# Cosine attention and a gated MLP on one core: loads put behind a reduction, a product moved to VectorE, gates changed, and identity products put between steps

## The chip, the cores and the metric

The kernel runs on one NeuronCore of a Trainium2 chip. Five engines work side by side: TensorE (PE in the profile, with its weight loads as PEld), VectorE (DVE), ScalarE (ACT), GpSimd (POOL) and SyncE (SP), which here issues most DMAs. Each engine works through its own instructions in program order and waits on semaphores for the others. The metric is the device time of one execution in microseconds; less is better. A measurement of this kernel tells a change of about 1% from none.

## The reference

Inputs: `q`, `k`, `v` of 8 batches, 12 heads, 448 positions and 64 features in float32, a scalar `tau` of 0.1, and two weights.

```python
q_n = q / (np.linalg.norm(q, axis=-1, keepdims=True) + 1e-06)
k_n = k / (np.linalg.norm(k, axis=-1, keepdims=True) + 1e-06)
attn = softmax(np.matmul(q_n, k_n.transpose(0, 1, 3, 2)) / tau)
x = np.matmul(attn, v).transpose(0, 2, 1, 3).reshape(3584, 768)
h = x @ w_in                 # 768 x 2048
out = (h * np.cos(h)) @ w_out    # 2048 x 768, float32
```

## The kernel before, in words

**Attention.** Four heads of one batch are a *quad*; there are 24, three to a batch. A quad's q and k are loaded (`load_qk`, L402, on SyncE's queue, 448 KB each, into a ring of three buffers `Qf`, `Kf`), squared and summed (`norm_a`, L510: squares on POOL, sums on DVE), turned into inverse norms and multiplied in (`norm_b`, L514), and transposed by DMA (`turn`, L541). V is loaded on POOL's queue (`load_v`, L408). For each of a quad's seven parts `scores` (L553) does four 64x64 products on TensorE into two PSUM banks, and ACT takes the exponential into `E`. `attend` (L583) multiplies `E` by V; after the seventh part DVE copies the PSUM result into `AVs` (L599), which frees the banks. The division by the row sums comes later. From quad 6 on, two quads at a time are summed by `round_` (L679): `sums` (L644) does it on TensorE, and `invert` (L660) takes 1/sum on ACT by a logarithm and an exponential into `Zs` (L664, L666), copies it by eight small DMAs on SyncE's queue to the partitions where it is needed, `R` (L672), and POOL multiplies `AVs` by `R` into `xT` (L675). Quads 0 to 5 do this in other ways (`spread`, `invert_spread`, `scale_x`: L603, L621, L634).

**MLP.** For each batch `c`, `m1_part` (L687) multiplies the first weight by `xT` (TensorE, 96 products of 448 columns), `m1` (L700) forms h cos h on ACT and DVE, and `m2` (L715) multiplies by the second weight; DVE copies the result to `osb` and SyncE stores it.

**Order.** The front, up to the first batch's `m1`, is written out by hand (L828 to L980). While it is recorded (`P.strict`) every instruction has a key, its number plus an entry of a table `MOVE` (L83), and each engine works in the order of the keys. TensorE's order is that of the keys all through. Behind the front, the other engines' order is chosen by a planner (L97 to L199), which simulates the engines with the durations and latencies written beside each operation. In a batch's `m2` the loop at L1047 alternates between attention of later quads and `m2`: a table `VISITS` (L749) says how many attention steps come next and how many `m2` products behind them, and `LATER` (L760) shifts the place of the attention product of the quad before in a quad's steps. `begin` (L768) is called as a quad's first scores are recorded: it makes the norms and transposes of quad+2, loads quad+4, and makes the squares of quad+3. A load with `after=` waits for the named operation; in the front the loads of quad 5 wait for the third of the four loads of the second weight, `half[3][:1]` (L930). `warm` (L819) issues products of an identity matrix with itself, which compute nothing that is used.

Of the kernel before, what the change touches and what calls it, by code (L numbers as in the profile page):

```python
# [21 lines left out]
class Planner:  # L22
# [13 lines left out]
    def __init__(self):  # L36
        self.ops = []
        self.last_write = {}
        self.readers = {}
        self.strict = False  # L40
        self.tail = {}

    def op(self, eng, dur, fn, r=(), w=(), after=(), dma=None, moves=0, mode="f", chain=None, keep=False, lead=0.0,
           packet=74, lock=False):
        o = Op()
# [3 lines left out]
        o.behind, o.lead, o.packet, o.lock = None, lead, packet, lock  # L49
        o.key = o.i + (self.MOVE.get(o.i, 0) if self.strict else 0)  # L50
        if keep or self.strict and eng in ("act", "dve", "pool", "sp"):
# [20 lines left out]
    def land(self, ring, issued, took, packet):  # L72
        s = max(issued + self.FIRST, self.ring[ring][0])
        for other, (until, theirs) in self.ring.items():
# [21 lines left out]

# [179 lines left out]
def bass_cosine_attention__then__act_gcu_kernel(  # L276
# [63 lines left out]
    def bank(i, n=S, p0=0, p1=128):  # L340
        return PS.ap()[p0:p1, 512 * i:512 * i + n]
# [4 lines left out]
    P = Planner()  # L346
    op = P.op
# [27 lines left out]
    def act(m, dur, fn, r=(), w=(), **kw):  # L375
        table(m)
        return op("act", dur, fn, r=[*r, "table"], w=w, **kw)
# [24 lines left out]
    def load_qk(qd, after=()):  # L402
        return [load_one(qd, w, after=after) for w in range(2)]
# [106 lines left out]
    def norm_a(qd):  # L510
        for w in range(2):
            square(qd, w, "pool")()
# [147 lines left out]
    def invert(quads, bk):  # L660
        z = 0
        np_ = 2 * len(quads)
        zz = Zs[z].ap()[0:32 * np_, :]
        act("exp", 0.44, lambda e: e.activation(zz, bank(bk, S, 0, 32 * np_), ACT.Ln, bias=0.0, scale=1.0),  # L664
            r=whole(bk), w=[("Zs", z)], lead=LEAD)
        act("exp", 0.47, lambda e: e.activation(zz, zz, ACT.Exp, bias=0.0, scale=-1.0), r=[("Zs", z)], w=[("Zs", z)], lead=LEAD)  # L666
        for i, qd in enumerate(quads):
            u, sl, b = qd % 2, qd % NA, qd // QB
            for r in range(2):
                for a in range(2):  # L670
                    src = bass.AP(Zs[z], (64 * i + 32 * r + 16 * a) * S, [[S, 16], [0, 4], [1, S]])
                    op("sp", 0.6, lambda e, r=r, a=a, u=u, src=src: e.dma_start(R[u].ap()[64 * r:64 * r + 64, a, :], src),  # L672
                       r=[("Zs", z)], w=[("R", u, r, a)], dma=("R", u, r, a), moves=0.5, packet=140, lead=LEAD)
            c0 = 2 * (qd % QB)
            op("pool", 2.04, lambda e, u=u, sl=sl, b=b, c0=c0: e.tensor_tensor(  # L675
                xT[b % 2].ap()[:, c0:c0 + 2, :], AVs[sl].ap(), R[u].ap(), ALU.mult),
                r=[("AV", sl), *(("R", u, r, a) for r in range(2) for a in range(2))], w=[("x", b % 2, qd % QB)], lead=LEAD, lock=True)

    def round_(quads, bk):  # L679
        sums(quads, bk)  # L680
        invert(quads, bk)

# [54 lines left out]
    def store(t, x0, x1, parts, engs=("sp", "sp")):  # L737
        so = t % 3
        for sg, eng in enumerate(engs):
# [9 lines left out]
    VISITS = [  # L749
# [7 lines left out]
        [],  # L757
        [],
    ]
    LATER = {18: -1, 5: 3, 7: -1, 21: -2, 9: 4, 10: -2, 12: -2, 23: 4, 15: -1, 8: 1, 22: -1, 17: -1, 14: 1}  # L760
    E1, E2 = NNB - 6, NNB - 4
# [3 lines left out]
    def now():  # L765
        return [[o for o in P.ops if o.eng == "pe"][-1]]

    def begin(qd):  # L768
        if qd + 2 < NQ:
            norm_b(qd + 2)  # L770
            turn(qd + 2)
        if qd < NQ - 4:
            load_qk(qd + 4)
        if qd + 3 < NQ:
            norm_a(qd + 3)

# [24 lines left out]
    def visit(slots):  # L801
        for kind, x in slots:
# [14 lines left out]
            scores(x, next_pair())  # L817

    def warm(n, bk=0, each=0.057):  # L819

        def mm(e):
            for _ in range(n):
                ins = e.matmul(bank(bk, 128), ident.ap(), ident.ap(), start=True, stop=True)
            return ins

        op("pe", each * n, mm, r=["ident"], w=whole(bk))

    P.strict = True  # L828
# [100 lines left out]
    scaled = scale(2, 1, "dve", HALVES[1])  # L929
    load_qk(5, half[3][:1])  # L930
    scale_x(0, X)
# [158 lines left out]
```

## Time and profile before

| what | us |
|---|---|
| three runs | 423.9, 425.42, 427.17 |
| their median | 425.42 |
| the profiled execution | 423.43 |
| its span | 421.6 |
| first scores on TensorE | 10.28 |
| first product of the first batch's `m1` | 34.66 |
| first product of the first batch's `m2` | 54.82 |
| first product of the third batch's `m1` | 147.33 |

A line of a timeline gives the start in us from the span's beginning, the duration of the group, the engine, the line of the kernel, the operation, what it writes and reads, the shape, and the number of instructions; in brackets stands how long the engine idled before it and whose work ended that. A line of the waits gives who waited for whom, then the sum, the number and the longest. SPq, ACTq and POOLq are the engines' DMA issues. A DMA in the chain of waits runs from its issue to its landing.

### The profile page before, as it was taken

The page shows a single profiled execution, that of the slowest core. Times are in us where ns is not written, and L with a number is a line of the kernel's source. Part 1 is how long each engine was busy: PE and PEld are TensorE (multiplying, and loading weights), DVE is VectorE, ACT ScalarE, POOL GpSimd, SP SyncE. Part 2 cuts the span into 40 slices and gives each one's busy share as a digit, 9 for nine tenths or more (in the row PEclk, how much of TensorE's full clock was granted, in tenths as well). Part 3 has the DMA queues.
Part 4 walks back from the last instruction along what each step waited for, and adds up shares of the span by engine and source line. Part 5 has one row for each costly group of instructions (what it writes and reads, how often), then busy time and mean ns, then how long its engine had stood idle before and what let it go on. Part 6 is the DMA issues. An engine that isn't in the chain of part 4 may idle for free.

```text
span 421.6 us, 8578 instructions
## 1 busy us (share of the span) xinstructions
PE 408.4 (97%) x3611; PEld 216.0 (51%) x3611; DVE 269.2 (64%) x338; ACT 307.1 (73%) x412; POOL 204.8 (49%) x139
## 2 busy tenths in 40 slices
PE   7979999999999999999999999999999999999996
PEld 6645454445544445445555555455554555555563
DVE  5867797879852749753896459824793137836931
ACT  5998789988888867697778667698787747505700
POOL 3866339792478694659539782269303303000000
PEclk9999999999999999999999999999999999999999
DMA  8999998995199979498938991389604624031032
GB/s 271 239 238 210 239 243 226 191 219 127 10 222 172 299 164 226 78 184 166 213 109 191 145 323 40 58 155 224 138 0 82 146 54 92 1 76 37 0 76 75
DMA packets 71399, 62.83 MB, mean 149 GB/s; under 512 B 40512, under 2 KB 66368, under 8 KB 71360
## 3 DMA queue, kind: packets, MB, share of 16 engines
q1 hardware_dynamic: 60688, 50.09, 48.9%
q0 software_dynamic: 10240, 11.80, 17.5%
q8 instruction: 28, 0.46, 0.5%
q10 hardware_dynamic: 432, 0.39, 0.3%
q14 instruction: 11, 0.09, 0.1%
HBM read 45.61 MB, written 11.01 MB: 134 GB/s over the span
## 4 chain that ended last, share of the span: by engine, by line
PE 83%; ACT 8%; DMA 4%; SPq 2%; POOL 1%; DVE 1%; issue 0%
PE PS L693 34%; PE PS L721 32%; PE PS L563 7%; PE PS L590 6%; ACT E L571 4%; PE PS L651 3%; DMA R<-Zs 3%; PE PS L612 1%; ACT E L578 1%; POOL xT L675 1%; SPq L672 1%; DMA Kf<-in_k_dram 1%; SPq L399 1%; DVE osb L730 1%; ACT ar L629 1%; PE PS L528 1%
## 5 line engine op out<-in xcount | busy, mean ns | idle before, releaser
L721 PE MATMUL PS<-W,gT 128*128 128x384 bf16 x896 | 156.3, 327 | 0.0
L571 ACT ACTIVATE E<-PS 128x896 bf16<-128x896 f32 x161 | 136.9, 917 | 18.3 <-PE PS L563 17.5
L693 PE MATMUL PS<-xT,W 128*128 128x448 bf16 x768 | 147.0, 353 | 1.9 <-ACT qT L536 1.0
L721 PEld LDWEIGHTS PS<-W,gT 128*128 128x128 bf16 x896 | 83.5, 98 | 69.1 <-issue 15.6
L693 PEld LDWEIGHTS PS<-xT,W 128*128 128x128 bf16 x768 | 74.7, 98 | 72.3 <-POOL xT L675 1.3
L706 ACT ACTIVATE ar<-PS 128x896 int32<-128x896 f32 x64 | 58.2, 910 | 41.8 <-PE PS L693 41.5
L708 DVE SCALAR_TENSOR_TENSOR ar<-ar,PS 128x896 f32<-128x896 int32 x64 | 69.2, 1084 | 24.0 <-ACT ar L706 24.0
L730 DVE COPY osb<-PS 128x384 f32<-128x384 f32 x56 | 31.1, 556 | 69.9 <-PE PS L721 69.4
L712 DVE TENSOR_TENSOR gT<-PS,ar 128x896 bf16<-128x896 f32 x64 | 69.5, 1088 | 7.8 <-ACT ar L710 7.4
L710 ACT ACTIVATE ar<-ar 128x896 f32<-128x896 f32 x64 | 60.5, 947 | 15.7 <-DVE ar L708 15.5
L675 POOL TENSOR_TENSOR xT<-AVs,R 128x896 bf16<-128x896 f32 x18 | 37.6, 2087 | 41.5 <-DMA R<-Zs 41.5
L563 PE MATMUL PS<-qT,kT 64*64 64x448 bf16 x672 | 49.6, 359 | 3.5 <-ACT E L571 1.6
L499 POOL TENSOR_TENSOR Qn<-Qf,rr 128x896 bf16<-128x896 f32 x21 | 38.1, 1813 | 29.3 <-DVE rr L491 23.5
L451 POOL TENSOR_TENSOR sqq<-Qf 128x896 bf16<-128x896 f32 x21 | 35.3, 1679 | 32.3 <-DMA Qf<-in_q_dram 17.9
L451 POOL TENSOR_TENSOR sqk<-Kf 128x896 bf16<-128x896 f32 x21 | 37.2, 1772 | 21.1 <-DVE n L455 15.6
L590 PE MATMUL PS<-E,Vb 64*64 64x448 bf16 x672 | 37.3, 350 | 0.0
L599 DVE COPY AVs<-PS 128x896 f32<-128x896 f32 x21 | 22.9, 1090 | 18.3 <-PE PS L590 18.2
L455 DVE TENSOR_REDUCE n<-sqq 128x14 f32<-128x896 bf16 (+2 forms) x23 | 23.6, 1030 | 12.8 <-POOL sqq L451 11.8
L563 PEld LDWEIGHTS PS<-qT,kT 64*64 64x64 bf16 x672 | 16.4, 105 | 29.4 <-issue 10.7
L499 POOL TENSOR_TENSOR Kn<-Kf,rr 128x896 bf16<-128x896 f32 x18 | 30.4, 1686 | 0.0
L411 POOL DMA_DIRECT2D Vb<-in_v_dram x24 | 18.2, 757 | 18.0 <-PE PS L563 13.6
L455 DVE TENSOR_REDUCE n<-sqk 128x14 f32<-128x896 bf16 (+2 forms) x23 | 23.8, 1038 | 3.7 <-POOL sqk L451 3.6
(54 smaller groups left out, 199.9 us busy)
## 6 DMA issues: line engine op xcount, KB each, us to landing
out_dram<-osb SPq DMA_DIRECT2D x54, 192.0 KB, 3.7
Qf<-in_q_dram SPq DMA_DIRECT2D x23, 448.0 KB, 5.0
Kf<-in_k_dram SPq DMA_DIRECT2D x23, 448.0 KB, 6.3
R<-Zs SPq DMA_DIRECT2D x72, 112.0 KB, 3.0
Vb<-in_v_dram POOLq DMA_DIRECT2D x24, 224.0 KB, 6.5
W<-in_moe_w_in_dram POOLq DMA_DIRECT2D x4, 768.0 KB, 17.0
W<-in_moe_w_out_dram POOLq DMA_DIRECT2D x4, 768.0 KB, 26.7
qT<-Qn SPq DMA_TRANSPOSE x20, 3.8
```

Source lines behind the costliest of these rows:

```text
L451: op(eng, (1.68 if eng == "pool" else 1.05) * n, lambda e: e.tensor_tensor(dst, src, src, ALU.mult), r=cut(nm + "f", s, part), w=own, afte ...
L455: return op("dve", 0.07 + 0.95 * n, lambda e: e.tensor_reduce(out=n2.ap()[:, u, H * w:H * w + H] if part == ALL[0] else jr(n2, u, w, part) ...
L499: lambda e: e.tensor_tensor(n[0].ap()[:, j0:j1].rearrange("p j r d -> p r j d"), f[s].ap()[:, :, j0:j1], rb, ALU.mult),
L563: ins = e.matmul(bank(bs + r, S, 64 * a, 64 * a + 64), kT[u].ap()[64 * r:64 * r + 64, j, a, :], qT[u].ap()[64 * r:64 * r + 64, :, a, :], s ...
L571: act("exp", 0.81, lambda e: e.activation(E[es].ap(), two(bs), ACT.Exp, bias=0.0, scale=INV_TAU), r=pair(bs), w=[("E", es)], chain="E")
L590: ins = e.matmul(bank(bk + a, S, 64 * r, 64 * r + 64), Vb[vs].ap()[64 * a:64 * a + 64, r, j, :], E[es].ap()[64 * a:64 * a + 64, r, :], sta ...
L693: ins = e.matmul(bank(bk + i2), W1.ap()[:, i, 128 * nb:128 * nb + 128], xT[c % 2].ap()[:, i, :], start=(i == 0), stop=(i == NKC - 1))
L706: op("act", 0.815, lambda e: e.activation(ar[s].ap().bitcast(I32), two(bk), ACT.Identity, bias=0.25, scale=INV2PI), r=bs, w=[("ar", s)])
L708: op("dve", 1.005, lambda e: e.scalar_tensor_tensor(ar[s].ap(), ar[s].ap().bitcast(I32), -2.0 * math.pi, two(bk), ALU.mult, ALU.add), r=bs ...
L710: act("sin", 0.86, lambda e: e.activation(ar[s].ap(), ar[s].ap(), ACT.Sin, bias=GUARD * math.pi / 2.0, scale=GUARD), r=[("ar", s)], w=[("a ...
L712: op("dve", 1.01, lambda e: e.tensor_tensor(gT.ap()[:, 2 * pr:2 * pr + 2, col:col + S], two(bk), ar[s].ap(), ALU.mult), r=bs + [("ar", s)] ...
L721: ins = e.matmul(bank(bk, HW), gT.ap()[:, f, col:col + 128], W2.ap()[:, f, HW * h:HW * h + HW], start=(f == 0), stop=(f == NNB - 1))
```

## The change

- **Quad 14's loads.** `begin(10)` no longer records the loads of quad 14 and the squares of quad 13; they are kept back and recorded behind the inversion of quads 8 and 9, and the loads wait for its exponential (L666).
- **x of quad 8** is multiplied on DVE instead of POOL. The planner's figures for the R copies change with it.
- **Gates in front.** Quad 5's loads wait for the second load of the second weight instead of the third (`half[2][1:]`). The load of quad 3's V (operation 102) goes behind the four loads of the second weight in POOL's order; entry 209, a logarithm of quad 4's norm on ACT, is taken out of `MOVE`.
- **Identity products by a table.** `FILL` gives, for the number of an operation, how many identity products go right ahead of it on TensorE, the PSUM bank that they write, and whether each is one 128x128 product ("f") or a pair of 64x64 products ("q"). The entries stand ahead of the first transpose (24: 13), a transpose of q (42: 3), the first scores (56: 9), scores and transposes of quads 1 and 2 (137 to 157: 26 in all), a product of the first `m1` (246: 2) and one of the first `m2` (312: 1).
- **Order tables.** `VISITS` of batches 0 to 4 and `LATER` get other numbers.

```diff
     def op(self, eng, dur, fn, r=(), w=(), after=(), dma=None, moves=0, mode="f", chain=None, keep=False, lead=0.0,
-           packet=74, lock=False):
+           packet=74, lock=False, key=None):
+        if key is None:
+            self.count += 1
+            key = self.count - 1
+            if self.strict:
+                key += self.MOVE.get(key, 0)
+            if self.count - 1 in self.FILL:
+                self.idle(*self.FILL[self.count - 1], key - 0.01)
...
-        o.key = o.i + (self.MOVE.get(o.i, 0) if self.strict else 0)
+        o.key = key
...
-            80: 4.0, 73: 2.0, 59: 6.5, 31: 0.0, 141: -1.5, 161: 1.0, 209: -2.0, 167: -1.5, 194: -1.5, 211: -2.0,
-            107: -3.5, 39: -12.5, 109: -4.5, 177: -1.0, 101: -25.5, 40: 2.5}
+            80: 4.0, 73: 2.0, 59: 6.5, 31: 0.0, 141: -1.5, 161: 1.0, 167: -1.5, 194: -1.5, 211: -2.0, 107: -3.5,
+            39: -12.5, 109: -4.5, 177: -1.0, 101: -25.5, 40: 2.5, 102: 4.5}
+    FILL = {24: [13, 1, 'f'], 42: [3, 1, 'f'], 56: [9, 1, 'q'], 137: [1, 6, 'q'], 139: [10, 6, 'q'], 141: [4, 2,
+            'q'], 155: [6, 6, 'q'], 157: [5, 6, 'q'], 246: [2, 2, 'f'], 312: [1, 0, 'f']}
...
-        act("exp", 0.47, lambda e: e.activation(zz, zz, ACT.Exp, bias=0.0, scale=-1.0), r=[("Zs", z)], w=[("Zs", z)], lead=LEAD)
+        done = act("exp", 0.47, lambda e: e.activation(zz, zz, ACT.Exp, bias=0.0, scale=-1.0), r=[("Zs", z)], w=[("Zs", z)], lead=LEAD)
...
-                       r=[("Zs", z)], w=[("R", u, r, a)], dma=("R", u, r, a), moves=0.5, packet=140, lead=LEAD)
+                       r=[("Zs", z)], w=[("R", u, r, a)], dma=("R", u, r, a), moves=1.3 if qd == 8 else 0.45, packet=140, lead=LEAD)
...
-            op("pool", 2.04, lambda e, u=u, sl=sl, b=b, c0=c0: e.tensor_tensor(
+            op(*(("dve", 1.05) if qd == 8 else ("pool", 2.04)), lambda e, u=u, sl=sl, b=b, c0=c0: e.tensor_tensor(
...
+        return done
 
     def round_(quads, bk):
         sums(quads, bk)
-        invert(quads, bk)
+        gate = invert(quads, bk)
+        if quads[-1] in BEHIND.values():
+            while put_off:
+                put_off.pop(0)([gate])
...
     VISITS = [
-        [(0, 26), (3, 12), (3, 11), (3, 4), (3, 4), (3, 12), (3, 10), (3, 3), (3, 4), (3, 0), (3, 4), (3, 5), (1, 1)],
-        [(0, 22), (3, 7), (3, 16), (3, 11), (3, 0), (3, 16), (3, 11), (3, 8), (3, 0), (3, 0), (3, 16), (3, 8),
-         (3, 5), (3, 8), (1, 0)],
...
+        [(0, 25), (3, 12), (3, 12), (3, 4), (3, 4), (3, 12), (3, 10), (3, 3), (3, 4), (3, 0), (3, 4), (3, 5), (1, 1)],
+        [(0, 20), (3, 10), (3, 14), (3, 13), (3, 0), (3, 16), (3, 11), (3, 8), (3, 0), (3, 0), (3, 16), (3, 10),
+         (3, 3), (3, 7), (1, 0)],
...
-    LATER = {18: -1, 5: 3, 7: -1, 21: -2, 9: 4, 10: -2, 12: -2, 23: 4, 15: -1, 8: 1, 22: -1, 17: -1, 14: 1}
+    LATER = {18: -2, 5: 3, 7: -1, 21: -2, 9: 4, 10: -2, 12: -2, 23: 4, 15: -1, 13: -1, 22: -1, 8: 1, 16: -1}
...
+    BEHIND = {10: 9}
+    put_off = []
+
     def begin(qd):
+        assert not put_off or BEHIND.get(qd)
         if qd + 2 < NQ:
             norm_b(qd + 2)
             turn(qd + 2)
+        steps = []
         if qd < NQ - 4:
-            load_qk(qd + 4)
+            steps.append(lambda after=(): load_qk(qd + 4, after))
         if qd + 3 < NQ:
-            norm_a(qd + 3)
+            steps.append(lambda after=(): norm_a(qd + 3))
+        if qd in BEHIND:
+            put_off.extend(steps)
+        else:
+            for f in steps:
+                f()
...
+    def products(e, n, bk, mode="f"):
+        for _ in range(n):
+            if mode == "f":
+                ins = e.matmul(bank(bk, 128), ident.ap(), ident.ap(), start=True, stop=True)
+            else:
+                p = 64 * (bk % 2)
+                for a in range(0, 128, 64):
+                    ins = e.matmul(bank(bk, 128, a, a + 64), ident.ap()[p:p + 64, 0:64], ident.ap()[p:p + 64, :],
+                                   start=True, stop=True)
+        return ins
...
+    P.idle = lambda n, bk, mode, key: op("pe", 0.06 * n, lambda e: products(e, n, bk, mode), r=["ident"], w=whole(bk),
+                                         mode=mode, key=key)
...
-    load_qk(5, half[3][:1])
+    load_qk(5, half[2][1:])
```

More of the change, by code (lines that the diff above doesn't have):

```diff
@@ L41, in __init__ @@
         self.tail = {}
+        self.count = 0
     def op(self, eng, dur, fn, r=(), w=(), after=(), dma=None, moves=0, mode="f", chain=None, keep=False, lead=0.0,
-           packet=74, lock=False):
+           packet=74, lock=False, key=None):
[6 more added lines that the diff above has]
+                self.idle(*self.FILL[self.count - 1], key - 0.01)
         o = Op()
@@ L817, in visit @@
             scores(x, next_pair())
-    def warm(n, bk=0, each=0.057):
[L821 to L826, printed above, removed]
+    def products(e, n, bk, mode="f"):
[8 more added lines that the diff above has]
+        return ins
+    def warm(n, bk=0, each=0.057):
+        op("pe", each * n, lambda e: products(e, n, bk), r=["ident"], w=whole(bk))
+    P.idle = lambda n, bk, mode, key: op("pe", 0.06 * n, lambda e: products(e, n, bk, mode), r=["ident"], w=whole(bk),
+                                         mode=mode, key=key)
     P.strict = True
```

6 rows, old and new, of the table VISITS are left out of this document.

## The prediction

> **What bounds the kernel now.** I read the page first, then TensorE's waits, then the busy time by stretch, and last the timelines of the places where TensorE waits. The page:
>
> ```profile
> span 421.6 us, 8578 instructions
> ...
> PE 408.4 (97%) x3611; PEld 216.0 (51%) x3611; DVE 269.2 (64%) x338; ACT 307.1 (73%) x412; POOL 204.8 (49%) x139
> ```
>
> TensorE (PE) is busy for 408.4 of 421.6 us. All its idle time together is 13.2 us, so the waits have to be counted one by one. TensorE's waits after 54 us (in total, times, longest):
>
> ```profile
> PE PS L563 <- DVE AVs L599: 1.0, 1, 1.0
> PE PS L693 <- POOL xT L675: 0.9, 1, 0.9
> PE PS L612 <- ACT E L571: 0.4, 1, 0.4
> ```
>
> Three stretches of the kernel (after the bounds: length; busy us of PE, weight loads, DVE, ACT, POOL; clock; DMA):
>
> ```profile
> 10.00:34.00 24.00, 20.72 (x349) 12.22 (x349) 18.34 (x28) 23.13 (x38) 18.27 (x18) 1.00 1.11 235
> 54.00:88.00 34.00, 33.57 (x382) 16.22 (x380) 28.08 (x33) 32.26 (x46) 25.20 (x15) 1.00 1.00 211
> 150.00:418.00 268.00, 267.70 (x2136) 140.88 (x2136) 160.79 (x189) 176.52 (x222) 110.14 (x69) 1.00 0.53 117
> ```
>
> From 10 to 34 us ScalarE (ACT) is the bound: 23.13 of 24 us. From 54 to 88 us TensorE and ACT are both nearly full. From 150 to 418 us TensorE idles for 0.30 us in all: almost nothing is to be had there, though a worse order can lose there.
>
> The profiled execution took 423.43 us, its span of 421.6 and 1.83 around it. The three runs took 423.9, 425.42 and 427.17 us, so the profiled one is the fastest of four, 2.0 below the median of the three. The sum is made against 423.43; the median of all four, (423.9 + 425.42) / 2 = 424.66, stands 1.2 above it, and I add this 1.2 at the end.
>
> **Quad 14's loads and the x of quad 8.** TensorE ahead of the third batch's first products:
>
> ```profile
> 145.11 0.57 PE L563 MATMUL PS<-qT,kT 64*64 64x448 bf16 x8 [1.03 <-DVE AVs L599]
> ...
> 147.33 1.69 PE L693 MATMUL PS<-xT,W 128*128 128x448 bf16 x8
> 149.92 2.26 PE L693 MATMUL PS<-xT,W 128*128 128x448 bf16 x11 [0.90 <-POOL xT L675]
> ```
>
> The second wait, 0.90 us, is for x of quad 8, which GpSimd (POOL) makes. SyncE's issues, ACT's inverse that releases the copies into R, the chain of waits, and POOL:
>
> ```profile
> 136.38 0.59 SPq L399 DMA_DIRECT2D Qf<-in_q_dram  x1
> 137.01 0.58 SPq L399 DMA_DIRECT2D Kf<-in_k_dram  x1
> 137.69 5.66 SPq L672 DMA_DIRECT2D R<-Zs  x8
> ```
>
> ```profile
> 136.15 0.58 ACT L666 ACTIVATE Zs<-Zs 128x448 f32<-128x448 f32 x1
> ```
>
> ```profile
> 127.05 3.85 DMA R<-Zs
> ...
> 140.07 7.65 DMA R<-Zs
> ```
>
> ```profile
> 147.79 2.07 POOL L675 TENSOR_TENSOR xT<-AVs,R 128x896 bf16<-128x896 f32 x1 [1.72 <-DMA R<-Zs]
> ```
>
> The inverse is done at 136.73, and quad 14's two loads (448 KB each) are issued at 136.38 and 137.01, ahead of the eight R copies on the same queue. The last copy of quad 8 lands 7.65 us after its issue, at 147.72, where the round before needed 3.85 us. Put behind the inverse, the two loads (0.59 + 0.58 us of issue, and 896 KB) come out of the way. R then lands between 140.07 - 1.31 + 3.85 = 142.6 (the earlier round's landing, the issue 1.31 earlier by the gap from 136.38 to 137.69) and 147.72 (nothing gained); I take 143.9, 3.8 us earlier, the difference of the two landing times, because the loads are what the two rounds differ in. What is queued behind the moved loads are stores, and nobody waits for quad 14 itself: TensorE first does the third batch's products and the scores of quads 12 and 13.
>
> The product itself moves from POOL (2.07 us) to VectorE (DVE). The nearest rows there are the three products of the same shape with `ar` in R's place (duration ns min/median/max):
>
> ```profile
> L638 DVE TENSOR_TENSOR xT<-AVs,ar x3: 1081/1092/2453, 71.1 to 86.0; 128x896 bf16<-128x896 f32 x3
> ```
>
> So 1.09 us, at most 2.45. With R at 143.9, x is ready at about 145.0 to 147.4 instead of 149.86; it is needed at 149.02, where the 0.90 us begin. Value: **-0.90 us**, bounds 0 and -0.90; what is late next is nothing, as the products behind it are dense. POOL gets 2.07 us back; this is TensorE's only wait on POOL after 54 us, so they are worth nothing more.
>
> The first wait, 1.03 us, is for a PSUM bank that DVE empties:
>
> ```profile
> 142.97 1.09 DVE L455 TENSOR_REDUCE n<-sqk 128x14 f32<-128x896 bf16 x1 [1.50 <-POOL sqk L451]
> 143.97 1.08 DVE L599 COPY AVs<-PS 128x896 f32<-128x896 f32 x1
> ```
>
> The copy stands behind a norm's sum for which DVE idles 1.50 us until POOL has squared. The change moves quad 13's squares and sums in the program order behind the sums of quads 8, 9, and puts a DVE product of 1.09 us into the same stretch. The wait may vanish (-1.03), stay (0), or grow by the product (+1.06, if x stands in the copy's place). I take half of it gone, **-0.5**: one DVE operation leaves the place, one comes.
>
> **The front.** The first 13 us of TensorE, and DVE's copy that releases the first scores:
>
> ```profile
> 1.39 4.02 PE L823 MATMUL PS<-ident 128*128 128x128 bf16 x36 [1.39 <-DVE ident L352]
> ...
> 6.79 1.70 PE L823 MATMUL PS<-ident 128*128 128x128 bf16 x14
> 8.51 0.50 PE L528 MATMUL PS<-ident,Qn 128*128 128x128 bf16 x3
> ...
> 10.28 0.57 PE L563 MATMUL PS<-qT,kT 64*64 64x448 bf16 x8 [0.52 <-DVE qT L538]
> 10.78 1.35 PE L823 MATMUL PS<-ident 128*128 128x128 bf16 x21
> ...
> 12.37 0.62 PE L823 MATMUL PS<-ident 128*128 128x128 bf16 x8
> ```
>
> ```profile
> 9.80 0.42 DVE L538 COPY qT<-PS 128x512 bf16<-128x512 bf16 x1 [0.39 <-PE PS L528]
> ```
>
> One product costs (4.02 - 1.70) / 22 = 0.105 us before 8.5 us and (1.35 - 0.62) / 13 = 0.056 after 10.8: TensorE runs at half rate at first and never goes back. The table adds 13 + 3 + 9 products ahead of the first scores. At half rate the 13 end at 1.39 + 49 x 0.105 = 6.5 and the 14 behind them some 0.2 late, into a gap that ends at 8.51; the 3 then push the ten transposes by 0.26, and the 9 (0.95 us) push the first scores from 10.28 to 10.78: **+0.5**. At full rate the last four transposes need 4 x 0.05 = 0.2 us less and all products fit: **-0.2**. ACT, full from then on, passes either on to the end. The trace cannot say which: I take 0 and keep both ends. [...]
>
> [...]
>
> Quad 5's loads now wait for the second load of the second weight instead of the third:
>
> ```profile
> 45.47 0.37 SPq L399 DMA_DIRECT2D Kf<-in_k_dram  x1
> 49.57 0.37 SPq L399 DMA_DIRECT2D Qf<-in_q_dram  x1
> ```
>
> ```profile
> 56.97 1.68 POOL L451 TENSOR_TENSOR sqq<-Qf 128x896 bf16<-128x896 f32 x1 [11.53 <-DMA Qf<-in_q_dram]
> ```
>
> They can start up to 3.7 us earlier (SyncE is free from 45.84), and POOL's square with them. TensorE's only wait between 54 and 88 us is the 0.4 for ACT, so this gains nothing directly. Quad 3's V goes behind the four loads of the second weight on POOL's queue. The first use of that weight and the first of this V:
>
> ```profile
> 54.82 4.39 PE L721 MATMUL PS<-W,gT 128*128 128x384 bf16 x26
> ...
> 67.60 1.49 PE L590 MATMUL PS<-E,Vb 64*64 64x448 bf16 x28
> ```
>
> The weight has to be there from 54.82 on, V at 67.60, so V has up to 12.8 us of room behind it; cost 0. Should the room be gone, TensorE stops for as long as V is late.
>
> **The order tables.** The first visit comes after 25 products instead of 26, so ACT, the co-bound there, starts earlier by 0.16, and the 0.4 us wait may go: -0.2 taken, bounds -0.6 and +0.4. The other changed fills and the five moved attention products shift work between places where TensorE is full; 0 taken, bounds -0.30 (all idle time after 150) and +1.0 (one new wait like that of 1.03).
>
> **The sum:** 423.43 - 0.90 - 0.5 + 0 - 0.2 + 0 = 421.8; with the 1.2 of the runs, **423.0**.
>
> **The rivals.**
> - *All of it, and an even front.* Unbroken work in front makes TensorE fast early, in every execution. Both waits go, the 0.42 before 88 us too: 423.43 - 0.90 - 1.03 - 0.42 - 0.20 = 420.9, and the 1.2 between runs is gone if the half rate in front is what sets the runs apart. For it: the half rate holds for some 10 us although TensorE is busy for most of them. Against: the profiled run, half rate until then, is the fastest of four. [...]
> - *The waits only change places.* DVE has no free place at 142 to 146, the copy stays late, the new order opens as much as it closes: 423.43 + 1.2 = 424.6. For it: 0.30 us of idleness in 268 us say that there is no slack for a loss to hide in.
> - *DVE stands still for R.* DVE works in program order. If x of quad 8 is put ahead of the copy at 143.97 and R lands where it does now, DVE waits until 147.72, multiplies until 148.8 and copies until 149.9; TensorE gets its bank at 149.95 instead of 145.11. That is +4.84 - 0.90 = +3.9, with the 1.2: 428.6; with the 2.45 us product 430.0. It decides once R lands later than 143.97 minus 1.09, so from 142.9 on it costs as much as R is late (at 143.9 the +1.06 above). For it: R landed at 147.72; against: the loads that held it are moved away.
>
> **How the numbers follow.** Within 1% of 425.42 (421.17 to 429.67) is about what a measurement of this kernel can tell from no change. Forecast 0.50 (its own range 421.6 to 425.0), all of it 0.22, change of places 0.18, DVE still 0.10. Faster by over 1%: the 0.22 and 0.03 of the forecast's low end, 0.25. Slower by over 1%: half of the last rival, 0.05. Within: 0.70. The range 420.4 to 427.0 reaches from below the first rival to the forecast with all its losses (0.5 in front, 1.0 in the order, 0.5 + 1.06 at the copy: 426.1) and the runs' own spread, and leaves out the last rival and the thin end below.
>
> **What would show it.** R's last copy of quad 8 lands near 143.9, and the chain no longer runs through R there; DVE's product takes 1.1 us and TensorE has no wait at the third batch's first products (step one). The wait for `AVs` near 145 is under 0.5 (step two). First scores between 10.1 and 10.8, and the rate of the 14 products near 7 us tells which end (step three). A new wait of over 0.5 us on TensorE after 54 us, or a median under 421 with an unchanged profile, would make the prediction wrong.

## The result, and the profile after

| | before | after |
|---|---|---|
| median of 22 runs each, us | 425.43 | 421.98 |
| lowest and highest | 423.24, 427.53 | 421.19, 425.82 |
| the profiled execution | 423.43 | 422.46 |
| its span | 421.6 | 420.6 |

The ratio of the times is 0.9929 with a 95% interval of 0.9910 to 0.9947: faster by 0.5 to 0.9%, small, but clear of the noise of these runs. The ratios, here and below, leave out runs of more than 1.5% above a kernel's fastest; in E7 below those are eight of twelve, so its ratio says nothing of its median. The two profiled executions differ by 1.0 us only, the medians by 3.45. So the gain has two parts: one that every profile can show, and one that lies in how the runs differ from each other.

The page of the kernel after, its span and engines:

```profile
span 420.6 us, 8751 instructions
...
PE 410.1 (97%) x3700; PEld 219.2 (52%) x3700; DVE 271.6 (65%) x339; ACT 308.0 (73%) x412; POOL 203.2 (48%) x138
```

TensorE is 1.7 us busier by its 89 further products and has 2.7 us less idle time (10.5 against 13.2). The waits of TensorE after 54 us (in total, times, longest):

```profile
PE PS L622 <- ACT E L581: 0.4, 1, 0.4
PE PS L573 <- issue: 0.4, 1, 0.4
PE PS L573 <- DVE AVs L609: 0.2, 1, 0.2
```

The line numbers are 9 to 14 higher than before (scores at L573, the copy of `AVs` at L609, x at L685, the first weight's products at L707). The wait for x, 0.9 us, is gone, and so is the wait for `AVs` near 145 us, 1.0 us: the 0.2 that is left stands at 71.3 us, ahead of another quad's scores. TensorE ahead of the third batch's first products, and DVE and POOL around x of quad 8 (timelines: start, duration, engine, line, what; idle time before it in brackets):

```profile
144.84 1.06 PE L573 MATMUL PS<-qT,kT 64*64 64x448 bf16 x12
145.83 1.31 PE L735 MATMUL PS<-W,gT 128*128 128x384 bf16 x7
147.07 0.38 PE L573 MATMUL PS<-qT,kT 64*64 64x448 bf16 x4
147.39 9.82 PE L707 MATMUL PS<-xT,W 128*128 128x448 bf16 x51
```

```profile
142.45 1.09 DVE L465 TENSOR_REDUCE n<-sqk 128x14 f32<-128x896 bf16 x1
144.18 1.09 DVE L609 COPY AVs<-PS 128x896 f32<-128x896 f32 x1 [0.64 <-PE PS L600]
...
145.67 1.03 DVE L685 TENSOR_TENSOR xT<-AVs,R 128x896 bf16<-128x896 f32 x1
```

```profile
145.84 2.40 POOL L509 TENSOR_TENSOR Qn<-Qf,rr 128x896 bf16<-128x896 f32 x1 [0.58 <-DVE rr L501]
148.21 1.68 POOL L509 TENSOR_TENSOR Kn<-Kf,rr 128x896 bf16<-128x896 f32 x1
```

The 51 products of the third batch run in one piece. DVE's copy no longer stands behind a sum that waits for POOL: it idles 0.64 us for TensorE itself, so the bank is freed as early as it can be. It starts no earlier than before, though (144.18 against 143.97): TensorE's product ahead of it ends later too, at 144.12 instead of 142.66. x of quad 8 is ready at 146.70, while the eight products ahead of its use (1.69 us before) end at about 149.1. Beside it, POOL's product took 2.40 us where the next one, alone, took 1.68. The R copies from issue to landing, after and then before (the same stretch, 136 to 152 us):

```profile
DMA to landing us min/median/max: 3.1/3.9/4.5
```

```profile
DMA to landing us min/median/max: 6.1/7.5/8.6
```

The fourth and last copy of quad 8 was issued at 139.84 and landed at 143.29. The chain of waits from 130 to 150 us, by line:

```profile
by line: PE PS L735 35.5%; PE PS L600 20.4%; PE PS L573 18.6%; PE PS L707 12.8%; PE PS L661 7.2%; DVE AVs L609 5.5%; issue 0.3%
```

No R copy is on it any more, and nothing of POOL; what is left beside TensorE is DVE's copy of `AVs`. The front:

```profile
1.39 4.84 PE L846 MATMUL PS<-ident 128*128 128x128 bf16 x49 [1.39 <-DVE ident L362]
...
6.78 1.11 PE L846 MATMUL PS<-ident 128*128 128x128 bf16 x17
...
10.20 0.57 PE L573 MATMUL PS<-qT,kT 64*64 64x448 bf16 x8
```

17 products in 1.11 us are 0.065 each: the full rate was there before 7 us, where before it came only at 10.08. The first scores came 0.08 earlier. By the starts of TensorE's stages, after minus before: first scores -0.08, first batch's `m1` +0.36 (35.02), second batch's `m1` +1.04 (89.10), third batch's `m1` +0.06 (147.39), third batch's `m2` -1.02 (165.56), and -1.0 from there to the end. So 55 to 89 us cost 0.68, 89 to 147 us gave 0.98 and the third batch's `m1` gave 1.08. The +0.68 belongs to that execution: from the first `m1` to the second it took 54.1 us, and 53.25 in three kernels below whose program is the same there (E6, E11, and E1 but for three identity products); before it took 53.40.

### The profile page after: what moved, and what is told of

Read it like the earlier page. It is cut to its first block, busy times and chain, and to the rows that moved or that the text cites. A ratio compares the mean times of both kernels' runs of the same rounds, so it can differ in the third digit from the quotient of the medians.

```text
span 420.6 us, 8751 instructions
## 1 busy us (share of the span) xinstructions
PE 410.1 (97%) x3700; PEld 219.2 (52%) x3700; DVE 271.6 (65%) x339; ACT 308.0 (73%) x412; POOL 203.2 (48%) x138
## 4 chain that ended last, share of the span: by engine, by line
PE 80%; DMA 11%; POOL 2%; DVE 2%; ACT 2%; SPq 1%; issue 1%
PE PS L735 33%; PE PS L707 30%; DMA W<-in_moe_w_out_dram 8%; PE PS L573 7%; PE PS L600 6%; PE PS L661 3%; DMA Qf<-in_q_dram 3%; SPq L555 1%; POOL E L461 1%; ACT E L581 1%; POOL W L436 1%; DVE n L465 1%; DVE AVs L609 1%; POOL sqq L461 0%; DVE osb L744 0%
## 5 line engine op out<-in xcount | busy, mean ns | idle before, releaser
L707 PE MATMUL PS<-xT,W 128*128 128x448 bf16 x768 | 146.8, 353 | 0.3 <-ACT qT L546 0.3
L707 PEld LDWEIGHTS PS<-xT,W 128*128 128x128 bf16 x768 | 74.7, 98 | 70.4 <-issue 0.6
L685 POOL TENSOR_TENSOR xT<-AVs,R 128x896 bf16<-128x896 f32 x17 | 35.5, 2088 | 41.4 <-DMA R<-Zs 41.3
L573 PE MATMUL PS<-qT,kT 64*64 64x448 bf16 x672 | 49.1, 358 | 2.6 <-ACT E L581 1.2
L609 DVE COPY AVs<-PS 128x896 f32<-128x896 f32 x21 | 22.9, 1090 | 19.5 <-PE PS L600 19.4
L573 PEld LDWEIGHTS PS<-qT,kT 64*64 64x64 bf16 x672 | 16.6, 105 | 26.4 <-issue 10.0
L600 PEld LDWEIGHTS PS<-E,Vb 64*64 64x64 bf16 x672 | 19.2, 107 | 13.1 <-ACT E L581 1.8
```

What stands on the lines that cost most here:

```text
L573: ins = e.matmul(bank(bs + r, S, 64 * a, 64 * a + 64), kT[u].ap()[64 * r:64 * r + 64, j, a, :], qT[u].ap()[64 * r:64 * r + 64, :, a, :], s ...
L600: ins = e.matmul(bank(bk + a, S, 64 * r, 64 * r + 64), Vb[vs].ap()[64 * a:64 * a + 64, r, j, :], E[es].ap()[64 * a:64 * a + 64, r, :], sta ...
L685: op(*(("dve", 1.05) if qd == 8 else ("pool", 2.04)), lambda e, u=u, sl=sl, b=b, c0=c0: e.tensor_tensor(xT[b % 2].ap()[:, c0:c0 + 2, :], A ...
L707: ins = e.matmul(bank(bk + i2), W1.ap()[:, i, 128 * nb:128 * nb + 128], xT[c % 2].ap()[:, i, :], start=(i == 0), stop=(i == NKC - 1))
```

## The experiments

Each kernel ran 12 times, one run of it profiled, beside the kernel before on the same chip. Besides the times, each run lists the mean clock that TensorE was granted. A run at 0.997 or below is called low here: 3.41 us at half rate, the length of the stretch in E3's profile, make 3.41 x 0.5 / 421 = 0.004, so 0.996 is one such stretch, 0.992 two. The other runs are called runs at full clock, though a late start of the full rate does not show in this mean (last section). In the table, "to before" is the difference of the medians in the same session, and a median of 12 runs can be off by some 0.5 us (an estimate: the medians of before in three sessions of 35 runs were 425.40, 424.96 and 424.55).

| | kernel | median (lowest, highest) | to before | ratio, 95% interval | low runs |
|---|---|---|---|---|---|
| | after | 421.98 (421.19, 425.82) | -3.45 | 0.9929, 0.9910-0.9947 | 2 of 22 |
| E1 | after without `FILL` | 424.01 (421.03, 426.60) | -1.39 | 0.9981, 0.9948-1.0013 | 8 of 12 |
| E2 | before with `FILL` | 424.03 (422.40, 427.26) | -1.37 | 0.9994, 0.9966-1.0022 | 3 of 12 |
| E3 | before with quad 14's part | 427.01 (422.98, 429.85) | +1.61 | 1.0026, 0.9993-1.0060 | 9 of 12 |
| E4 | after with the old gates | 422.92 (421.91, 425.86) | -2.48 | 0.9970, 0.9943-0.9997 | 3 of 12 |
| E5 | after, early fills only | 421.93 (421.00, 424.17) | -3.03 | 0.9945, 0.9919-0.9971 | 3 of 12 |
| E6 | after, x of quad 8 on POOL | 422.09 (420.99, 425.14) | -2.87 | 0.9967, 0.9943-0.9991 | 3 of 12 |
| E7 | after, quad 14's loads back | 429.91 (421.28, 433.24) | +4.95 | 0.9993, 0.9946-1.0041 | 9 of 12 |
| E8 | after with the old order tables | 424.57 (422.73, 426.18) | +0.02 | 0.9994, 0.9962-1.0027 | 1 of 12 |
| E9 | after, late fills only | 422.59 (421.12, 424.12) | -2.37 | 0.9958, 0.9935-0.9980 | 3 of 12 |
| E10 | after without quad 14's part | 422.73 (421.58, 425.12) | -1.82 | 0.9965, 0.9934-0.9996 | 1 of 12 |
| E11 | after, a POOL square put behind | 421.23 (421.00, 422.53) | -3.32 | 0.9921, 0.9892-0.9950 | 0 of 12 |
| E12 | after, that square put ahead | 422.27 (421.05, 425.98) | -2.28 | 0.9946, 0.9911-0.9980 | 4 of 12 |

Of the kernel before, 61 of 105 runs of these sessions were low. Runs at full clock compared with each other take the low runs out of the medians: before 423.35, 423.18 and 422.97 in the three sessions (14, 15 and 15 runs), after 421.94 (20 runs). So about 1.0 to 1.4 us of the 3.45 are there without any low run, and the rest goes with their number.

**E1, no identity products from the table.**

```diff
-    FILL = {24: [13, 1, 'f'], 42: [3, 1, 'f'], 56: [9, 1, 'q'], ...}
+    FILL = {}
```

> The changed kernel with an empty table of identity products. Theory A (the two waits near 145 give about 2 us in every run, and the products in front even out the runs by keeping TensorE's clock up): lowest time about 421.2 as with the table, but runs spread over some 4 us again, median about 423.5, the slow ones with a mean clock below 0.99. Rival B (the products buy nothing, all of the gain is the waits): median about 422.0 with the spread of the changed kernel, 421.2 to 422.8.

The median is 2.0 us higher and 8 of 12 runs are low (four at 0.996, four at 0.990 to 0.992), though the lowest run, 421.03, is as low as any of after. Its four runs at full clock have a median of 422.19, after's twenty 421.94. So, as far as four runs can show, the fills do not speed up a run at full clock; they keep the runs from falling to half rate.

**E2, the fills alone on the kernel before.** The table and its code are put into the kernel before, all else stays.

> The kernel before with the table of identity products and nothing else. Theory A: lowest about 423.2 as before, median pulled down to about 423.7, hardly a run with a clock below 0.99. Rival B: median 425.4, spread 423.2 to 427.5 as before. Rival C (the products delay the front): lowest above 423.6.

Low runs went from 21 of 35 to 3 of 12, as in E1 seen from the other side, and the median fell by 1.4. The ratio does not tell it from no change. The nine runs at full clock have a median of 423.55, before's 423.35: again the fills gain nothing there. Over all kernels that carry the whole table 26 of 118 runs were low (9 of these in E7), over before, E1 and E3, which carry none of it, 78 of 129.

Its profile shows something else. TensorE's waits after 54 us, complete:

```profile
PE PS L573 <- ACT E L581: 0.4, 1, 0.4
PE PS L622 <- ACT E L581: 0.4, 1, 0.4
PE PS L573 <- DVE AVs L609: 0.4, 1, 0.4
```

The order, the loads and the x of quad 8 are those of before, and yet there is no wait for x, and 0.4 us for `AVs` (near 145 us) instead of 1.0. The R copies took 5.6 us in the median, not 7.5. So the two waits of 0.9 and 1.0 us, on which the change was planned, belonged in part to the one execution of before that was profiled.

**E3, quad 14's part alone on the kernel before**: loads and squares behind the inversion, x of quad 8 on DVE, the new planner's figures for the copies, old order tables, no fills, old gates.

```diff
+    BEHIND = {10: 9}
...
-            op("pool", 2.04, ...
+            op(*(("dve", 1.05) if qd == 8 else ("pool", 2.04)), ...
```

> The kernel before with quad 14's loads put back, x of quad 8 on DVE and the planner's figure for it, nothing else. Theory A: both waits near 145 gone or nearly, about 1.9 us less than before in like runs: lowest about 421.3, median about 423.5 with the spread of before. Rival (the waits only change places without the new order tables): lowest 422.3 or more, a new wait of 0.5 us or more between 88 and 150 us.

Its profiled execution gained 1.2 us between 89 and 147 and 1.1 in the third batch's `m1`, like after, and lost them again. TensorE's waits after 54 us:

```profile
PE PS L572 <- DMA kT<-Kn: 1.1, 1, 1.1
PE PS L706 <- DVE gT L725: 1.0, 1, 1.0
```

Both waits are new: one for a later quad's transposed k, which ends at 188.9 us, one for h cos h, at 259.5. That is the rival in which the waits only change places, though not between 88 and 150 us, where it looked for them. The same profile shows the clock falling (length of the stretch; busy us and instructions of PE, weight loads, DVE, ACT, POOL; clock; DMA):

```profile
24.30:27.70 3.40, 2.02 (x28) 1.05 (x25) 3.40 (x6) 3.40 (x5) 2.29 (x2) 1.00 1.15 254
27.75:31.15 3.40, 3.40 (x39) 1.69 (x41) 1.52 (x3) 2.77 (x4) 1.34 (x1) 0.50 1.16 208
31.15:34.50 3.35, 2.42 (x56) 1.24 (x52) 0.81 (x1) 2.78 (x4) 1.01 (x2) 1.00 1.15 213
```

and the same first stretch in the kernel after:

```profile
24.30:27.70 3.40, 3.10 (x67) 2.04 (x65) 2.89 (x6) 3.40 (x6) 3.29 (x2) 1.00 1.14 256
```

In E3 DVE and ACT are full from 24.3 to 27.7 and TensorE is busy for 2.02 us, in gaps of at most 0.64; from 27.73 to 31.15 the clock is 0.50, and the 39 products take the whole stretch. In after, the table puts 26 fills (pairs) before 34 us, and TensorE is busy for 3.10 us there.

Before's profile has the same products with the same gaps of 0.55, 0.19 and 0.64 us, from 23.0 to 26.0 us, and kept its clock. In E3 the drop comes 13.65 us behind the rise to the full rate at 14.08, four times the 3.41 us that the low stretch lasts. Windows of 3.41 us counted from the rise have a border at 24.32 in E3, just ahead of the first of these gaps; in before, counted from its rise at 10.08, at 23.74, just behind it. That this sets the two apart is an estimate; no run shows it.

**E4, the old gates in front.**

```diff
-    load_qk(5, half[2][1:])
+    load_qk(5, half[3][:1])
```

(with entry 209 back and 102 out of `MOVE`.)

> The changed kernel with the gates of before: quad 5's loads wait for the third load of the second weight, quad 3's V ahead of it, entry 209 back. Theory: quad 5's loads, waiting at the head of SyncE's queue, hold up quad 7's loads and so quad 4's transposes; with the old gate the transposes land 2 us earlier, the wait of TensorE near 65.7 us goes, and the time is 0.5 us less, about 421.4. Rival: the gates gain or do nothing, 422.0 or more.

The old gates came out 0.9 us slower by the median, not faster; the intervals of this ratio and of after's touch (0.9943, 0.9947), so the size is rough. The nine runs at full clock have a median of 422.87, 0.9 above after's as well. In the profile the wait near 65.7 us did not go: TensorE waits 0.41 us for ACT there, 0.37 in after.

**E5 and E9, the fills by halves.** E5 keeps the entries 24, 42 and 56 (ahead of the first scores), E9 those from 137 on.

> The changed kernel with only the products ahead of the first scores (entries 24, 42, 56). Theory: they bring TensorE's full rate before 8 us in every run, but not the drop to half rate for 3.4 us near 28 us that one profile showed behind a window in which TensorE worked for 0.37 of the time; so about a third to a half of the runs have a mean clock of 0.997 or less, the median is about 422.8, and the runs at full clock stay within 421.2 to 423. Rival (the early ones are all that matters): median 422.0, at most 2 of 12 runs below 0.997.

> The changed kernel with only the later products (entries 137 to 312). Theory: hardly a run with a mean clock of 0.997 or less, but the full rate comes at 10 or 14 us in part of the runs, which the mean clock does not show; runs at a clock of 1.0 spread from 421.2 to 424 and the median is about 422.8. [...]

Either half brought the low runs to 3 of 12. E5's median is level with after's, not 0.8 above it; E9's is 0.6 above it, near what was expected but hardly more than the half us by which a median can be off. (The 0.37 in E5's expectation counts columns streamed, as in the last section; by time TensorE was busy for 2.02 of 3.40 us of that window.) What differs is the clock of the low runs: all three of E5 at 0.996, all three of E9 at 0.991 to 0.992. In E9's profile the full rate came at 14.13 us and the first `m1` at 36.02, a whole us later than in after. In the ten profiles that have the early entries the full rate was there by 7.42 us at the latest; in the four without them (before, E1, E3, E9) it came at 10.08, 4.37, 14.08 and 14.13. So both halves do something, at two places, and how much each is worth is not settled.

**E6, x of quad 8 back on POOL.**

```diff
-            op(*(("dve", 1.05) if qd == 8 else ("pool", 2.04)), ...
+            op("pool", 2.04, ...
```

> The changed kernel with x of quad 8 on POOL again. Theory: what removed the wait of 0.90 us is R landing at 143.3 instead of 147.7; POOL is done with x by 148.5 at the latest, TensorE needs it at 149.0, so no change: about 422.0, no wait of TensorE for x. Rival (the move to DVE is needed): a wait of 0.5 us or more for x, 422.6 or more.

TensorE's waits after 54 us, complete:

```profile
PE PS L622 <- ACT E L581: 0.3, 1, 0.3
PE PS L573 <- issue: 0.2, 1, 0.2
```

No wait for x: with the loads out of the way R is early enough for POOL's 2 us as well. The median is 0.1 above after's. The move to DVE is worth nothing that could be measured.

**E7, the loads back in front of the copies**, x of quad 8 still on DVE.

```diff
-    BEHIND = {10: 9}
+    BEHIND = {}
```

> The changed kernel with quad 14's loads and quad 13's squares back in front, x of quad 8 still on DVE. Theory: R lands near 147.7, DVE waits for it in its order; if x stands behind the copy that frees the banks, x is ready 1.0 us earlier than on POOL and the time is about 422.2; if it stands ahead of the copy, TensorE waits 3 us or more near 145, 425 or more. The prediction's third rival is the second.

TensorE, DVE and POOL in the profiled execution (timelines):

```profile
150.34 1.69 PE L707 MATMUL PS<-xT,W 128*128 128x448 bf16 x8
154.96 5.28 PE L707 MATMUL PS<-xT,W 128*128 128x448 bf16 x27 [2.93 <-DVE xT L685]
```

```profile
150.61 4.29 DVE L685 TENSOR_TENSOR xT<-AVs,R 128x896 bf16<-128x896 f32 x1
```

```profile
148.98 1.69 POOL L461 TENSOR_TENSOR sqk<-Kf 128x896 bf16<-128x896 f32 x1
150.62 1.69 POOL L509 TENSOR_TENSOR Qn<-Qf,rr 128x896 bf16<-128x896 f32 x1
152.26 1.68 POOL L509 TENSOR_TENSOR Kn<-Kf,rr 128x896 bf16<-128x896 f32 x1
153.91 2.94 POOL L685 TENSOR_TENSOR xT<-AVs,R 128x896 bf16<-128x896 f32 x1
```

TensorE waits 2.93 us for x, but not by the mechanism of the rival that foresaw a loss here: the copy of `AVs` had already run at 147.14, ahead of x, so nothing stood still for R. DVE's product itself took 4.29 us instead of 1.03. It began while POOL's square was still running (until 150.67); POOL's `Qn` and `Kn` followed that square without a gap and kept their 1.69 and 1.68 while DVE crawled. TensorE's waits list one more loss, 1.1 us for h cos h near 213 us. Something like it happened in front, where DVE's second product of Qn ran into POOL's square:

```profile
7.96 3.24 DVE L509 TENSOR_TENSOR Qn<-Qf,rr 128x384 bf16<-128x384 f32 x2
```

```profile
8.95 1.69 POOL L461 TENSOR_TENSOR E<-Kf 128x896 bf16<-128x896 f32 x1
```

Two products that took 3.24 us here took 1.15 where POOL's square came later (E11 below). TensorE then waited 2.18 us, and the clock followed:

```profile
7.05:10.46 3.41, 1.60 (x25) 1.26 (x23) 3.41 (x5) 2.12 (x10) 3.12 (x3) 1.00 1.08 347
10.46:13.87 3.41, 2.61 (x33) 1.71 (x34) 2.98 (x5) 0.49 (x1) 3.41 (x6) 0.50 1.16 171
```

The lowest run, 421.28 at a full clock, is as fast as after's: the edit does not cost in every run. Whether that run was free of collisions is not known, as it was not profiled. The front is the same in both programs, so why 9 of these 12 runs were low and 2 of 22 of after is not explained by the edit. What the two profiles show is that POOL's V loads, which wait for a load of q, began at 7.32 us in E7 and at 8.65 in after, so that the square behind them began at 8.95 instead of 10.28. That is not enough for a collision: in E9's profile the square began at 8.81, and DVE's two products took 1.15 us.

**E8, the old order tables in the kernel after.** `VISITS` and `LATER` get their old numbers.

> The changed kernel with VISITS and LATER of before. Theory: quad 14's loads put back lead to new waits in the old order (the profile of that change alone shows 1.1 us for a transpose near 221 us and 1.0 us near 292 us); with all else as changed they stay, so about 2 us more than the changed kernel, 424.0. Rival (the tables are worth nothing): 422.0.

The median is 2.6 above after's, and level with before. TensorE's waits after 54 us:

```profile
PE PS L707 <- DVE gT L726: 0.9, 1, 0.9
PE PS L573 <- DMA kT<-Kn: 0.8, 1, 0.8
```

These are the two waits of E3, here ending at 185.9 and 256.4 us (the 221 and 292 of the expectation are not the places that the traces show). After, with the new tables and all else the same, has neither.

**E10, quad 14's part undone**: `BEHIND = {}`, x of quad 8 on POOL, the old figure for the copies; new tables, gates and fills.

> The changed kernel with everything about quad 14 undone: its loads and quad 13's squares in front, x of quad 8 on POOL, the planner's figures of before. Theory: R lands near 147.7 again, TensorE waits 0.9 us for x of quad 8 and up to 1.0 us for the banks near 145: runs at full clock about 423.5, median about 424. Rival (the wait is hidden by the new tables): 422.3 or less.

TensorE's waits after 54 us, the first three:

```profile
PE PS L707 <- POOL xT L685: 0.3, 1, 0.3
PE PS L573 <- issue: 0.3, 1, 0.3
PE PS L573 <- DVE AVs L609: 0.2, 1, 0.2
```

The fourth R copy of quad 8 was issued at 140.49 and landed at 146.03, 2.7 us later than in after and 1.7 earlier than before, and TensorE waits only 0.3 us for x. The 0.2 for `AVs` stands at 70.2 us; near 145 there is none. So most of both waits was absent without quad 14's part. Whether the new order, the gates and the fills did that is not shown, as E2 has little of these waits with the old order and the old gates. Undoing the part costs 0.75 us by the medians and 1.6 against the sessions' own before; its interval and after's overlap.

**E11, POOL's square of quad 1's k waits for DVE's two products of Qn too.**

```diff
-    for part in HALVES:
-        scale(0, 0, "dve", part)
+    qs = [scale(0, 0, "dve", part) for part in HALVES]
...
-    add1 = [square(1, 1, "pool", after=[kept])]
+    add1 = [square(1, 1, "pool", after=[kept, *qs])]
```

> The changed kernel in which POOL's square of quad 1's K waits for DVE's two products of quad 0's Q as well. Theory: now and then the two collide (one profile shows the DVE product at 2.77 us instead of 0.69, and first scores at 12.4 instead of 10.2), and then the clock drops too; kept apart, no run is above 424 for that reason, and the time is otherwise the same: median 421.8. Rival (the collision is no cause of spread, or the wait costs): 422.0 or more with runs at 425 as before.

```profile
8.02 1.15 DVE L509 TENSOR_TENSOR Qn<-Qf,rr 128x384 bf16<-128x384 f32 x2
```

```profile
9.46 1.69 POOL L461 TENSOR_TENSOR E<-Kf 128x896 bf16<-128x896 f32 x1
```

The products end at 9.17 and the square starts at 9.46. In this profile it would have started there anyway, as POOL issues its V loads until 9.44; so the profile does not show the new wait at work. All 12 runs lie between 421.00 and 422.53, none is low; the 22 of after spread over 4.6 us. It is faster than before (0.9892 to 0.9950) and has the lowest median of all; that it is faster than after is not shown, since the intervals overlap, and none of 12 low against 2 of 22 is no difference to build on.

**E12, the same square put ahead of the second V load**, to provoke the collision: entry 49 of `MOVE` 0.5 instead of 2.0.

> The changed kernel in which the same square stands ahead of the second V load in POOL's order, so that it starts where DVE's product of quad 0's Q runs. Theory: the two collide in most runs, the product takes 2 to 3 us, first scores come near 12 us: 2 us or more above the changed kernel, 424 or more, and clocks below 0.997 in more than half of the runs. Rival (POOL waits and DVE goes on, as in most profiles): 422.0, first scores at 10.2.

Four of 12 runs were low and the median was 422.27. In the profile quad 1's k landed only at 9.57, so the square started behind the products all the same and nothing collided. How often products collide in front is not measured.

## Why the prediction was right, and where not

The forecast of 423.0 us held the median of 421.98 within its range; -2.4 was forecast from the median shown and -3.45 came. The number came out well partly by luck. The steps that were summed give 1.6 us in every run, and the two profiles differ by 1.0, runs at full clock by 1.0 to 1.4; the rest of the 3.45 came from the low runs becoming few, which the sum had at 0.

- **x of quad 8, -0.90: right between the two profiles (-1.08), for the first half of its reason only.** R landed at 143.29 where 143.9 was forecast, by copies of 3.9 us in the place of 7.5, and TensorE has no wait there. The move to DVE, costed in the same step, was not needed (E6). And E10, without the moved loads, has only 0.3 of this wait, E2, without any of the step, none: the 0.90 was the wait of one execution, costed as if every run had it.
- **The wait for `AVs`, -0.5: the size half, the mechanism not shown.** 89 to 147 us gave 0.98, and the copy does not stand behind a late sum any more. But E10 has no such wait near 145 without the moved squares, and E1 (0.68) and E11 (0.45) keep part of it with them. What sets this wait from one execution to the next was not found.
- **DVE's product, 1.09 us and at most 2.45: 1.03 in after, but the upper bound was too low.** It took 4.29 with POOL's products beside it (E7). I had read the 2.45 as spread; the trace of before has POOL's square beside it, begun 0.17 us earlier (last section).
- **The fills, 0: mis-sized by about 2 us.** The first scores moved by -0.08, inside the bounds, and no wait shortened. But E1 shows that they are worth 2.0 in the median, by keeping TensorE from half-rate stretches that 58% of before's runs had and its profiled execution did not. (In the two profiles that show such a stretch it lies in the front; where it lies in the other runs is not recorded.) The sum has nothing for the later fills; E3's rows show a drop behind a stretch with gaps of at most 0.64 us.
- **The gates, 0:** E4 has them at 0.9, just at the edge of what the intervals show.
- **The order tables, -0.2: mis-sized.** Once quad 14's loads are moved, the old tables cost 2.6 us (E8), with two new waits of 0.9 and 0.8 that E3 shows as well. The bounds of -0.3 and +1.0 were made from the idle time before the change, where these waits did not exist.
- **The 1.2 us that the runs lay above the profile: this carry-over failed.** After's median lies 0.5 below its profile. The 1.2 was treated as a constant of the measurement; it was the mark of the low runs, and the change made them few. Before's runs at full clock have medians of 422.97 to 423.35, at its profile's 423.43.

Of the rivals, "all of it, and an even front" (420.9) had the right mechanism between the runs and comes within 1.1 us; the argument against it, that the profiled run with its late full rate is the fastest of four, looked at the late start of the full rate and missed the later drop. "The waits only change places" is E3 and E8, the change without its tables. "DVE stands still for R" happened in no profile here; in E7 DVE was slow for another reason.

The values of the single parts do not add up to 3.45: 2.0 for the fills, 0.9 for the gates and 2.6 for the tables are already 5.5. That undoing one part leaves the others tuned to it is a likely reason, but no run shows it.

The half rate was costed in front alone, as before's profiled execution "never goes back" to it; those of E3 and E7 did. The half-rate stretch in E3 lasts 3.41 us (from 27.73 to 31.15), that in E7 6.83 us, twice as long (from 10.46), and neither came behind an idle TensorE: it was busy for 2.02 of the 3.40 us before the drop in E3, for 1.60 of 3.41 in E7.

What stays open: why E7 had so many low runs; the value of each half of the fills; how often DVE and POOL collide in front; what quad 14's part is worth, as the waits that it was made for differ from one execution to the next; and why a few of before's runs at a full clock take 427 us, since none of these was profiled.

## What to carry to other kernels

Where a kernel's runs scatter by a per cent and its profile shows nothing, read the clock of every run before the waits of one: here 61 of before's 105 runs were low and its profiled one was not, and in E3's profile 3.41 us at half rate followed a stretch in which TensorE was busy for 2.02 of 3.40 us. A wait that one profile shows is not yet a wait of every run: profile the kernel before more than once, or a variant of it that leaves that place alone. A load moved out of the way of small copies can open new waits behind it until the order of the work there is made again (1.1 and 1.0 us in E3, 0.9 and 0.8 in E8). A VectorE product with two operands in SBUF took 4.29 us beside GpSimd's products (E7) and 1.03 to 1.09 mostly; one that TensorE waits for is worth keeping apart from them.

## What the runs showed of the hardware

**The clock fell behind sparse stretches, with TensorE busy for 2.02 of 3.40 us (E3) and 1.60 of 3.41 (E7).** Count the columns that TensorE streamed in each window of 3.41 us (the length of E3's half-rate stretch), the windows laid on the changes of the clock, at the rate that makes the densest windows 0.99 to 1.00. The windows before a drop come out at 0.37 (E3, 24.32 to 27.73) and 0.36 (E7, 7.05 to 10.46); windows at 0.39 and 0.41 (E1) and 0.47 (before) were followed by no drop. While the clock was low, no rise followed windows of 0.72 (E3) and 0.77 (E5), and one followed a window of 0.78 (before). These shares are estimates that move by some hundredths with how a product's columns are laid over its record, so they put the windows in order but place no border. The profile's busy time does not even order them: 1.60 us (E7) and 2.02 (E3) before the two drops, 1.61 and 2.02 in E1's two windows without one. The full rate first came at 4.2 us (E12) to 14.1 us (E3, E9). That late start does not show in a run's mean clock: the profiled execution of before reached the full rate at 10.08 us and has a mean clock of 1.000, that of E9 at 14.13 us and 0.999, where 10 us at half rate, counted in, would take off 10 x 0.5 / 421 = 0.012.

**DVE products with two SBUF operands and POOL products ran slower side by side: DVE's took up to 4.29 us instead of 1.03, POOL's up to 2.59 instead of 1.68.** 128x896 on DVE: 1.03 to 1.09 us mostly, 4.29 in E7, where POOL kept its 1.69. In after it was POOL that lost, 2.40 against 1.68, while DVE kept 1.03. The 2.45 us of the product in before stood beside a square of POOL:

```profile
86.03 2.45 DVE L638 TENSOR_TENSOR xT<-AVs,ar 128x896 bf16<-128x896 f32 x1
```

```profile
85.86 1.67 POOL L451 TENSOR_TENSOR sqq<-Qf 128x896 bf16<-128x896 f32 x1
87.50 2.52 POOL L451 TENSOR_TENSOR sqk<-Kf 128x896 bf16<-128x896 f32 x1
```

POOL's first square began first and kept its time, and DVE's product grew by about what was left of it; POOL's next square began while DVE's product ran, and grew in turn. So it is in every overlap of such products in the profiles of before and after: where DVE's product of 128x896 began first (seven times), it took 1.03 to 1.09 us and POOL's 2.40 to 2.59; where it began beside a product of POOL that was already running (six times), it took 1.20 to 2.45. DVE's products of the same size with one operand in PSUM, `gT<-PS,ar`, took 1.08 to 1.09 us in all 39 overlaps with POOL's products in the two profiles. E7 at 150 us fits it, with POOL's products in a row ahead of DVE. E7's front does not: there DVE's second product began 0.52 us before the square and took 2.77 us.

**Two loads of 448 KB ahead of small copies on the same queue went with a longer latency of the copies**: medians of 7.5 us (before), 6.1 (E7) and 5.6 (E2, E10) with the loads ahead, 3.1 to 4.2 in the ten profiles in which the loads had moved behind (3.9 in after).
